# Decode attention on one core: a longer lag between scores and P·V, a plain load for q, and a loop on TensorE

## The chip, the cores and the metric

The kernel runs on one core of one Trainium2 chip. The metric is the device time of one execution in microseconds (us). Before the change the kernel took 352.61 us, the median of 4 runs (350.58 to 353.67 us). A profile is one further execution, recorded by the hardware; its span is 1.8 to 1.9 us shorter than the measured time of the same execution.

Engines are named as the profile names them: PE is TensorE (PEld its weight loads), DVE is VectorE, ACT is ScalarE, POOL is GpSimd, SP is SyncE. A trailing q (SPq, ACTq) means that engine's sequencer.

## The reference

```python
B, Hq, Hkv, Sq, Sk, D = 8, 32, 4, 4, 8192, 128        # bf16 inputs
k = jnp.repeat(k, Hq // Hkv, axis=1)
v = jnp.repeat(v, Hq // Hkv, axis=1)
scores = jnp.einsum("bhqd,bhkd->bhqk", q, k) * D ** -0.5
p = softmax(scores, axis=-1)
return jnp.einsum("bhqk,bhkd->bhqd", p, v)
```

Each batch has 128 query rows (32 heads x 4) in four groups of 32 that share a K/V head. K and V together are 134.22 MB and are read once; everything else is small.

## The kernel before

K and V come in 64 loads of 2,097,152 bytes ("units"), 32 each, all issued from SP. A unit holds 4 "chunks" of 512 positions for all four K/V heads; a batch has 16 chunks. There are four K buffers and four V buffers. For each chunk, PE transposes K (`ktp`), DVE and ACT each copy half of it out of PSUM (`kte`), PE computes scores (`qk`), and DVE scales them into SBUF and keeps a running minimum of the negated scores (`ev`). After 16 chunks of a batch its maximum is known (`negmax`), and the second half can begin: ACT computes the exponentials (`exp`), PE transposes them (`tp`), DVE copies (`ptc`), PE multiplies by V (`pv`).

The second half of a batch runs one batch, 16 chunks, behind its first half, so K is loaded 16 chunks ahead of V:

```python
for c in range(NCH):                      # NCH = 16
    steps.append((None, c))
for b in range(B):
    for c in range(NCH):
        n2 = b * NCH + c                                    # chunk of the second half
        n1 = (b + 1) * NCH + c if b + 1 < B else None       # chunk of the first half
        steps.append((n2, n1))
...
for (n2, n1) in steps:                    # order of the loads
    if n1 is not None and n1 % CPU == 0: dma_order.append(("k", n1 // CPU))
    if n2 is not None and n2 % CPU == 0: dma_order.append(("v", n2 // CPU))
...
# SP: a buffer is refilled when PE is done with what it held
if kind == "k":
    if m >= NK:  s.wait_ge(sem_pe_ktp, NPAIR * ((m - NK) * CPU + CPU))
    s.dma_start(Kn[ks][:, :, :], k[...]).then_inc(sem_k[ks], 16)
else:
    if m >= NVU: s.wait_ge(sem_pe_pv, (m - NVU) * CPU + CPU)
    s.dma_start(Vu[vs][:, :, :], v[...]).then_inc(sem_v[vs], 16)
...
# ACT, at the start: q is transposed by the DMA
for b in range(B):
    a.dma_start_transpose(QT[:, b, :], q[b].rearrange("h s d -> (h s) d")).then_inc(sem_q, 16)
...
# PE: the first score matmul waits for all of q (until 20.84 us in the profile); the K transposes behind it go on at 21.46 us
if first_qk[0]: t.wait_ge(sem_q, 16 * B)
...
# PE, after the last K: four chunks' transposes, then four chunks' P.V
for ui in range(0, len(tail_chunks), CPU):
    grp = tail_chunks[ui:ui + CPU]
    for n2 in grp:
        if n2 not in tp_done: emit_tp(n2)
    for n2 in grp: emit_pv(n2)
```

Of the kernel before, what the change touches and what calls it, by code (L numbers as in the profile page):

```python
# [5 lines left out]
dt = mybir.dt  # L6
# [5 lines left out]
def bass_standalone__gqa_softmax__sampling_kernel(  # L12
# [13 lines left out]
    P = 128  # L26
# [10 lines left out]

    NK = 4
# [4 lines left out]
    NPS = 16  # L43
    NTP = 2
    NPTS = 12
    GPB = 2
    NPAIR = G // GPB
    assert NPAIR == 2

# [3 lines left out]
    with ExitStack() as es:  # L53
# [5 lines left out]
        QT = sb("QT", [P, B, P], dt.bfloat16)  # L59
        Kn = [sb(f"Kn{i}", [P, G, JJ * D], dt.bfloat16) for i in range(NK)]  # L60
        Vu = [sb(f"Vu{i}", [P, G, JJ * D], dt.bfloat16) for i in range(NVU)]
        KT = [sb(f"KT{i}", [P, G, CH], dt.bfloat16) for i in range(NKT)]
        S_sb = sb("S", [P, Sk], dt.float32)
        Pb = [sb(f"P{i}", [P, CH], dt.bfloat16) for i in range(NPS)]
        PTs = [sb(f"PTs{i}", [P, CH], dt.bfloat16) for i in range(NPTS)]
# [10 lines left out]
        KT_ps = [ps_t(f"KTps{i}", [P, GPB, CH], dt.bfloat16) for i in range(NKTB)]  # L76

        sem_setup = sem("setup")
        sem_q = sem("qdma")
        sem_k = [sem(f"kdma{i}") for i in range(NK)]  # L80
# [16 lines left out]

        def kte_count(i):
            return i // NPAIR + 1

        steps = []
        for c in range(NCH):
            steps.append((None, c))
        for b in range(B):
            for c in range(NCH):
                n2 = b * NCH + c
                n1 = (b + 1) * NCH + c if b + 1 < B else None
                steps.append((n2, n1))
        NSTEPS = len(steps)
# [4 lines left out]
        def n1_of(t):  # L114
            return steps[t][1] if 0 <= t < NSTEPS else None

        TAIL_T = next((t for t, (n2, n1) in enumerate(steps) if n1 is None and n2 is not None), NSTEPS)

        def qk_deferred(n1):
            return (n1 % NCH) != NCH - 1  # L120

        def ktp_hoisted(t):
            if t <= 0 or t >= NSTEPS:
                return False
            n2, n1 = steps[t]
            return n1 is not None and n2 is not None and (n2 % NCH) == 0
# [30 lines left out]
        def _(s):  # L157
            for kind, m in dma_order:
# [19 lines left out]
        def _(t):  # L178
            t.wait_ge(sem_setup, 2)

            def emit_ktp(n1, pair):
# [3 lines left out]
                if cc == 0 and pair == 0:  # L185
                    t.wait_ge(sem_k[ks], 16 * (m // NK + 1))
                qi = n1 * NPAIR + pair
                qs = qi % NKTB
                if qi >= NKTB:
                    prev = qi - NKTB  # L190
                    if prev % NPAIR == 0:
                        t.wait_ge(sem_dve_kte, kte_count(prev))
                    else:
                        t.wait_ge(sem_act_kte, kte_count(prev))
# [11 lines left out]
            first_qk = [True]  # L206

            def emit_qk(n1):
                b, c = bc(n1)
                kt = n1 % NKT  # L210
                ss = n1 % NSP
                if first_qk[0]:
                    t.wait_ge(sem_q, 16 * B)
                    first_qk[0] = False
                t.wait_ge(sem_dve_kte, kte_count(n1 * NPAIR + 0))
                t.wait_ge(sem_act_kte, kte_count(n1 * NPAIR + 1))
                if n1 >= NSP:
                    t.wait_ge(sem_dve_p1, n1 - NSP + 1)
                for g in range(G):
                    ins = t.matmul(  # L220
                        S_ps[ss][32 * g:32 * (g + 1), :],
                        lhsT=QT[:, b, 32 * g:32 * (g + 1)],
# [6 lines left out]
            def emit_tp(n2):  # L229
                psl = n2 % NPS  # L230
                ts = n2 % NTP
                t.wait_ge(sem_act, n2 + 1)
                if n2 >= NTP:
                    t.wait_ge(sem_dve_pt, n2 - NTP + 1)
# [8 lines left out]
            def emit_pv(n2):  # L243
# [6 lines left out]
                t.wait_ge(sem_dve_pt, n2 + 1)  # L250
                if cc == 0:
                    t.wait_ge(sem_v[vs], 16 * (m // NVU + 1))
                if c == 0 and b >= 1:
                    t.wait_ge(sem_dve_fin, 3 * (b - 1) + 3)
# [14 lines left out]
            pending_qk = None  # L269
            tp_done = set()  # L270
            for ti in range(TAIL_T):
                n2, n1 = steps[ti]
                hoisted_here = ktp_hoisted(ti)
                if n1 is not None and not hoisted_here:
# [205 lines left out]
```

## Time and profile before

| | before |
|---|---|
| median time | 352.61 us |
| span of the profile | 351.2 us |
| K and V | 134.22 MB, 64 loads |
| GB/s in the middle (50 to 320 us) | 407 to 408 |
| busy share PE / DVE / ACT | 75% / 65% / 63% |

The first lines are from the page: the span; busy time by engine; what the DMA moved in 40 equal slices of the span (8.8 us each); then queues, with packets, MB, and the time their packets took as a share of 16 DMA engines' span. Queue q1 carries K and V, q10 the DMA transposes of q, and q8 instructions in packets of 16 KB.

```profile
span 351.2 us, 12106 instructions
...
PE 261.9 (75%) x5120; PEld 206.4 (59%) x5120; DVE 227.9 (65%) x544; ACT 222.3 (63%) x385; POOL 5.2 (1%) x14
...
GB/s 262 375 349 379 413 406 407 408 407 409 408 408 408 408 411 407 407 410 407 409 408 410 409 406 411 409 407 406 411 411 404 409 408 410 407 409 406 350 239 7
...
q1 hardware_dynamic: 33792, 134.22, 96.3%
q8 instruction: 41, 0.67, 0.8%
q10 hardware_dynamic: 1280, 0.26, 0.4%
```

No compute engine is above 75%, and the DMA moves a flat 408 GB/s from slice 6 to slice 37. The kernel is limited by its loads; the GB/s line falls off only at its two ends. The table of time windows looks closer there. Its columns are the window, its length, busy us (and instructions) of PE, PEld, DVE, ACT and POOL, the granted PE clock, the mean DMA share and GB/s.

```profile
4.00:8.78 4.78, 0.00 (x0) 0.00 (x0) 0.00 (x0) 0.00 (x0) 0.00 (x0) 1.00 1.06 338
...
22.00:26.30 4.30, 4.30 (x49) 3.33 (x47) 2.81 (x7) 1.88 (x2) 0.00 (x0) 1.00 0.81 323
26.30:30.70 4.40, 4.40 (x72) 3.30 (x69) 4.32 (x12) 3.24 (x4) 0.00 (x0) 1.00 0.94 344
...
200.00:300.00 100.00, 78.20 (x1528) 61.87 (x1525) 69.15 (x167) 66.79 (x118) 1.62 (x3) 0.91 1.03 408
...
325.00:330.00 5.00, 4.45 (x103) 3.29 (x101) 4.21 (x11) 3.78 (x5) 0.00 (x0) 0.96 0.87 348
330.00:335.00 5.00, 2.79 (x24) 1.54 (x28) 2.74 (x9) 3.56 (x11) 0.54 (x1) 0.72 0.98 376
335.00:338.00 3.00, 2.84 (x73) 2.38 (x73) 0.98 (x3) 3.00 (x10) 0.00 (x0) 0.50 0.76 309
338.00:340.00 2.00, 1.69 (x45) 1.26 (x46) 1.15 (x3) 2.00 (x7) 0.00 (x0) 0.74 0.55 215
```

Early, 338 GB/s at a DMA share above 1 (1.06) means that the DMA engines were busy. From 22 to 31 us the share falls to 0.81 and 0.94: the DMA had run short of issued loads, the fifth K load being issued only at 25.4 us. At the back the rate falls step by step.

The chain of work that ended last shows the end of the kernel (start in us, length in us, what):

```profile
331.44 7.79 ACT P L432 x21
...
339.32 2.83 ACT P L432 x8
...
346.50 1.10 PE acc L258 x64
...
347.68 0.36 DVE osb L368
...
348.32 0.54 POOL out_dram L149
```

After the last K, the 16 exponentials of the last batch run one after another on ACT; only then come the last transposes, P·V, normalization and store.

### The profile page before, as it was taken

What the parts mean: (1) busy time and instruction counts of PE and PEld (TensorE: products, weight loads), DVE (VectorE), ACT (ScalarE), POOL (GpSimd) and SP (SyncE); (2) the same over time, 40 slices, a digit from 0 to 9 for tenths busy, and PEclk for the clock granted to TensorE, in tenths of its full rate; (3) what the DMA queues carried; (4) which work ended last, traced back from release to release, by engine and by line L of the source; (5) the groups of instructions that cost most, each with busy time, mean ns of one, the idle gap of its engine ahead of it and who ended that gap; (6) DMA issues with size and microseconds to landing.
All of it is one profiled execution on the core that took longest, in us unless ns stands there. A gap on an engine that the chain in (4) does not pass through costs nothing.

```text
span 351.2 us, 12106 instructions
## 1 busy us (share of the span) xinstructions
PE 261.9 (75%) x5120; PEld 206.4 (59%) x5120; DVE 227.9 (65%) x544; ACT 222.3 (63%) x385; POOL 5.2 (1%) x14
## 2 busy tenths in 40 slices
PE   0469988886867979786698776978687879696774
PEld 0347666665645757564576655766565657475463
DVE  0139978876755778576758675777575686575743
ACT  0327697857756478485749575775575766665690
POOL 0000000000000000000000000000000000000000
PEclk9999999999988899899969998899899898988868
DMA  8999999999999999999999999999999999999950
GB/s 262 375 349 379 413 406 407 408 407 409 408 408 408 408 411 407 407 410 407 409 408 410 409 406 411 409 407 406 411 411 404 409 408 410 407 409 406 350 239 7
DMA packets 35380, 135.51 MB, mean 386 GB/s; under 512 B 2432, under 2 KB 2432, under 8 KB 35328
## 3 DMA queue, kind: packets, MB, share of 16 engines
q1 hardware_dynamic: 33792, 134.22, 96.3%
q8 instruction: 41, 0.67, 0.8%
q10 hardware_dynamic: 1280, 0.26, 0.4%
q0 software_dynamic: 256, 0.26, 0.2%
q14 instruction: 11, 0.09, 0.1%
HBM read 134.22 MB, written 0.26 MB: 383 GB/s over the span
## 4 chain that ended last, share of the span: by engine, by line
DMA 82%; PE 9%; ACT 3%; ACTq 3%; issue 1%; SPq 1%; DVE 1%; POOL 0%; DVEq 0%
DMA Vu<-in_v_dram 79%; PE KTps L199 5%; ACT P L432 3%; DMA QT<-in_q_dram 3%; ACTq L407 3%; PE Sps L220 2%; PE acc L258 1%; PE PTps L236 1%; SPq L164 1%; DVE PTs L351 0%; DVE KT L320 0%; POOL out_dram L149 0%; DVE osb L368 0%; DVE S L331 0%; DVE negmax L341 0%
## 5 line engine op out<-in xcount | busy, mean ns | idle before, releaser
L418 ACT ACTIVATE KT<-KTps 128x1024 bf16<-128x1024 bf16 x128 | 130.9, 1023 | 97.0 <-PE KTps L199 94.3
L199 PE MATMUL KTps<-ident,Kn 128*128 128x128 bf16 x2048 | 149.2, 231 | 14.4 <-DMA Kn<-in_k_dram 10.1
L199 PEld LDWEIGHTS KTps<-ident,Kn 128*128 128x128 bf16 x2048 | 131.9, 104 | 20.0 <-issue 20.0
L331 DVE TENSOR_SCALAR_CACHE_REDUCE S<-Sps 128x512 f32<-128x512 f32 x128 | 88.6, 692 | 31.8 <-PE Sps L220 22.4
L320 DVE COPY KT<-KTps 128x1024 bf16<-128x1024 bf16 x128 | 88.4, 691 | 23.4 <-PE KTps L199 22.6
L432 ACT ACTIVATE P<-S,negmax 128x512 bf16<-128x512 f32 x128 | 91.3, 713 | 11.9 <-DVE negmax L341 11.9
L351 DVE COPY PTs<-PTps 128x512 bf16<-128x512 bf16 x128 | 53.7, 422 | 62.8 <-PE PTps L236 62.0
L258 PE MATMUL acc<-Vu,PTs 128*32 128x128 bf16 x2048 | 54.4, 231 | 47.4 <-DMA Vu<-in_v_dram 34.0
L258 PEld LDWEIGHTS acc<-Vu,PTs 128*32 128x32 bf16 x2048 | 41.4, 101 | 66.2 <-issue 51.4
L220 PE MATMUL Sps<-KT,QT 128*32 128x512 bf16 x512 | 54.0, 409 | 12.9 <-DMA QT<-in_q_dram 7.2
L236 PE MATMUL PTps<-ident,P 128*128 128x128 bf16 x512 | 54.4, 235 | 10.9 <-ACT P L432 8.4
L236 PEld LDWEIGHTS PTps<-ident,P 128*128 128x128 bf16 x512 | 31.5, 103 | 26.6 <-ACT P L432 11.4
L220 PEld LDWEIGHTS Sps<-KT,QT 128*32 128x32 bf16 x512 | 13.5, 93 | 28.2 <-DMA QT<-in_q_dram 7.4
L432 ACT ACTIVATION_READ_ACCUMULATOR P<-S,negmax 128x1 f32 x128 | 24.4, 191 | 0.0
L331 DVE DVE_READ_ACCUMULATOR S<-Sps 128x1 f32 x128 | 10.7, 83 | 0.0
L149 POOL DMA_DIRECT2D out_dram<-osb x8 | 4.5, 558 | 342.9 <-DVE osb L368 342.9
L418 ACT ACT_TABLE_LOAD x1 | 1.3, 1283 | 11.6 <-issue 11.6
L368 DVE TENSOR_SCALAR osb<-acc,rrec 128x128 bf16<-128x128 f32 x8 | 2.8, 351 | 1.5 <-PE acc L258 1.3
L341 DVE TENSOR_REDUCE negmax<-rminp 128x1 f32<-128x16 f32 x8 | 1.4, 170 | 0.3
L363 DVE RECIPROCAL rrec<-rsum 128x1 f32<-128x1 f32 x8 | 1.3, 164 | 0.3
L359 DVE TENSOR_REDUCE rsum<-rsump 128x1 f32<-128x16 f32 x8 | 1.3, 161 | 0.0
L141 POOL TENSOR_SCALAR_AFFINE_SELECT ident<-ident 128x128 bf16<-128x128 bf16 x1 | 0.3, 284 | 0.2 <-POOL ident L139 0.2
(5 smaller groups left out, 0.6 us busy)
## 6 DMA issues: line engine op xcount, KB each, us to landing
Kn<-in_k_dram SPq DMA_DIRECT2D x32, 2048.0 KB, 24.2
Vu<-in_v_dram SPq DMA_DIRECT2D x32, 2048.0 KB, 24.3
out_dram<-osb POOLq DMA_DIRECT2D x8, 32.0 KB, 4.8
QT<-in_q_dram ACTq DMA_TRANSPOSE x8, 8.7
```

Source lines behind the costliest of these rows:

```text
L149: gp.dma_start(out[b].rearrange("h s d -> (h s) d"), out_sb[b % 2][:, :]).then_inc(sem_out[b % 2], 16)
L164: s.dma_start(Kn[ks][:, :, :], k[b, :, u * KUNIT:(u + 1) * KUNIT, :].rearrange("g (p jj) d -> p g (jj d)", jj=JJ),).then_inc(sem_k[ks], 16)
L199: ins = t.transpose(KT_ps[qs][:, gl, j * P:(j + 1) * P], Kn[ks][:, g, jj * D:(jj + 1) * D], ident[:, :],)
L220: ins = t.matmul(S_ps[ss][32 * g:32 * (g + 1), :], lhsT=QT[:, b, 32 * g:32 * (g + 1)], rhs=KT[kt][:, g, :], start=True, stop=True, tile_po ...
L236: ins = t.transpose(PT_ps[ts][:, j * P:(j + 1) * P], Pb[psl][:, j * P:(j + 1) * P], ident[:, :],)
L258: ins = t.matmul(acc[32 * g:32 * (g + 1), 0:D], lhsT=PTs[tsb][:, j * P + 32 * g:j * P + 32 * (g + 1)], rhs=Vu[vs][:, g, jj * D:(jj + 1) * ...
L320: vv.tensor_copy(KT[kt][:, 0:GPB, :], KT_ps[qs][:, :, :]).then_inc(sem_dve_kte, 1)
L331: vv.tensor_scalar(S_sb[:, c * CH:(c + 1) * CH], S_ps[ss][:, :], -scale, None, ALU.mult, ALU.min, accum_out=rowmin_parts[bp][:, c:c + 1],) ...
L351: vv.tensor_copy(PTs[tsb][:, :], PT_ps[ts][:, 0:CH]).then_inc(sem_dve_pt, 1)
L407: a.dma_start_transpose(QT[:, b, :], q[b].rearrange("h s d -> (h s) d")).then_inc(sem_q, 16)
L418: a.activation(KT[kt][:, GPB:2 * GPB, :], KT_ps[qs][:, :, :], ACT.Copy).then_inc(sem_act_kte, 1)
L432: a.activation(Pb[psl][:, :], S_sb[:, c * CH:(c + 1) * CH], ACT.Exp, bias=negmax[bp][:, :], scale=-1.0, accum_out=rowsum_parts[bp][:, c:c ...
```

## The change

The intent is to shorten both ends. The lag grows from 16 to 24 chunks, so that six V loads follow the last K and hide the last exponentials. Scores are kept in a ring of 24 chunks; P and P-transposed buffers shrink to 8 each to pay for it. q comes by one plain load in front of the K loads and is transposed on PE. PE's middle part becomes a hardware loop of 6 trips over 16 steps, with waits that count up by the trip number. The core of the diff:

```diff
+    L = NCH + NCH // 2
+    NSS = L
-    NPS = 16
+    NPS = 8
-    NPTS = 12
+    NPTS = 8
...
+        NSTEPS = NTOT + L
         steps = []
-        for c in range(NCH):
-            steps.append((None, c))
-        for b in range(B):
-            for c in range(NCH):
-                n2 = b * NCH + c
-                n1 = (b + 1) * NCH + c if b + 1 < B else None
-                steps.append((n2, n1))
+        for t in range(NSTEPS):
+            n1 = t if t < NTOT else None
+            n2 = t - L if t >= L else None
+            steps.append((n2, n1))
...
+            s.dma_start(Qn, q.rearrange("b h s d -> (h s) b d")).then_inc(sem_q, 16)
...
+            t.wait_ge(sem_q, 16)
+            for b in range(B):
+                ins = t.transpose(QT_ps[:, b * P:(b + 1) * P], Qn[:, b, :], ident[:, :])
+            ins.then_inc(sem_qt, 1)
...
+            for ti in range(L):
+                step(ti)
+            with t.Fori(0, TRIPS) as trip:
+                loop[0] = trip
+                off[0] = trip * NCH
+                for ti in range(L, L + NCH):
+                    step(ti)
...
-            for b in range(B):
-                a.dma_start_transpose(
-                    QT[:, b, :], q[b].rearrange("h s d -> (h s) d")
-                ).then_inc(sem_q, 16)
```

Cut: a two-slot copy of the current batch's q (so that the loop body names fixed addresses), changed slot tables for K-transposed buffers, and the removal of special orders at batch ends.

More of the change, by code (lines that the diff above doesn't have):

```diff
@@ L48, in bass_standalone__gqa_softmax__sampling_kernel @@
     assert NPAIR == 2
+    assert B * D <= NPTS * CH
+    assert B * P <= 2 * CH
     NTOT = B * NCH
@@ L59, in bass_standalone__gqa_softmax__sampling_kernel @@
         QT = sb("QT", [P, B, P], dt.bfloat16)
+        QTc = sb("QTc", [P, 2, P], dt.bfloat16)
         Kn = [sb(f"Kn{i}", [P, G, JJ * D], dt.bfloat16) for i in range(NK)]
@@ L62, in bass_standalone__gqa_softmax__sampling_kernel @@
         KT = [sb(f"KT{i}", [P, G, CH], dt.bfloat16) for i in range(NKT)]
-        S_sb = sb("S", [P, Sk], dt.float32)
+        S_sb = sb("S", [P, NSS, CH], dt.float32)
         Pb = [sb(f"P{i}", [P, CH], dt.bfloat16) for i in range(NPS)]
-        PTs = [sb(f"PTs{i}", [P, CH], dt.bfloat16) for i in range(NPTS)]
+        PTs_all = sb("PTs", [P, NPTS, CH], dt.bfloat16)
+        PTs = [PTs_all[:, i, :] for i in range(NPTS)]
+        nq_slots = -(-(B * D) // CH)
+        Qn = PTs_all[:, 0:nq_slots, :].rearrange("p a c -> p (a c)")[:, 0:B * D].rearrange(
+            "p (b d) -> p b d", b=B
+        )
         rowmin_parts = [sb(f"rminp{i}", [P, NCH], dt.float32) for i in range(2)]
@@ L76, in bass_standalone__gqa_softmax__sampling_kernel @@
         KT_ps = [ps_t(f"KTps{i}", [P, GPB, CH], dt.bfloat16) for i in range(NKTB)]
+        QT_ps = S_ps[0][:, :].bitcast(dt.bfloat16)
         sem_setup = sem("setup")
         sem_q = sem("qdma")
+        sem_qt = sem("qt")
         sem_k = [sem(f"kdma{i}") for i in range(NK)]
@@ L96, in bc, with ktslot, ktprev, kslot @@
             return n // NCH, n % NCH
+        KSLOT = [i % NKTB for i in range(NPAIR * NCH - 2)] + [0, 1]
+        KTSLOT = [c % NKT for c in range(NCH - 1)] + [1]
+        def ktslot(n1):
+            return KTSLOT[n1 % NCH]
+        def ktprev(n1):
+            p = n1 - 1
+            while p >= 0 and ktslot(p) != ktslot(n1):
+                p -= 1
+            return p
+        def kslot(qi):
+            return KSLOT[qi % (NPAIR * NCH)]
+        def kprev(qi):
+            p = qi - 1
+            while p >= 0 and kslot(p) != kslot(qi):
+                p -= 1
+            return p
         def kte_count(i):
             return i // NPAIR + 1
+        NSTEPS = NTOT + L
         steps = []
-        for c in range(NCH):
-            steps.append((None, c))
-        for b in range(B):
-            for c in range(NCH):
-                n2 = b * NCH + c
-                n1 = (b + 1) * NCH + c if b + 1 < B else None
-                steps.append((n2, n1))
-        NSTEPS = len(steps)
+        for t in range(NSTEPS):
+            n1 = t if t < NTOT else None
+            n2 = t - L if t >= L else None
+            steps.append((n2, n1))
         def n2_of(t):
             return steps[t][0] if 0 <= t < NSTEPS else None
-        def n1_of(t):
-            return steps[t][1] if 0 <= t < NSTEPS else None
-        TAIL_T = next((t for t, (n2, n1) in enumerate(steps) if n1 is None and n2 is not None), NSTEPS)
-        def qk_deferred(n1):
-            return (n1 % NCH) != NCH - 1
-        def ktp_hoisted(t):
-            if t <= 0 or t >= NSTEPS:
-                return False
-            n2, n1 = steps[t]
-            return n1 is not None and n2 is not None and (n2 % NCH) == 0
+        TAIL_T = NTOT
+        tail_chunks = [steps[ti][0] for ti in range(TAIL_T, NSTEPS)]
+        tail_units = []
+        for n2 in tail_chunks:
+            if n2 // CPU not in tail_units:
+                tail_units.append(n2 // CPU)
         dma_order = []
@@ L179, in _ @@
             t.wait_ge(sem_setup, 2)
+            t.wait_ge(sem_q, 16)
+            for b in range(B):
+                ins = t.transpose(QT_ps[:, b * P:(b + 1) * P], Qn[:, b, :], ident[:, :])
+            ins.then_inc(sem_qt, 1)
+            loop = [None]
+            off = [0]
             def emit_ktp(n1, pair):
@@ L185, in emit_ktp @@
                 if cc == 0 and pair == 0:
-                    t.wait_ge(sem_k[ks], 16 * (m // NK + 1))
+                    t.wait_ge(sem_k[ks], 16 * (m // NK + 1) + off[0])
                 qi = n1 * NPAIR + pair
-                qs = qi % NKTB
-                if qi >= NKTB:
-                    prev = qi - NKTB
+                qs = kslot(qi)
+                prev = kprev(qi)
+                if prev // NPAIR >= n1 - 1 and prev >= 0:
                     if prev % NPAIR == 0:
-                        t.wait_ge(sem_dve_kte, kte_count(prev))
+                        t.wait_ge(sem_dve_kte, kte_count(prev) + off[0])
                     else:
-                        t.wait_ge(sem_act_kte, kte_count(prev))
+                        t.wait_ge(sem_act_kte, kte_count(prev) + off[0])
                 for gl in range(GPB):
@@ L204, in emit_ktp @@
                 ins.then_inc(sem_pe_ktp, 1)
-            first_qk = [True]
             def emit_qk(n1):
                 b, c = bc(n1)
-                kt = n1 % NKT
+                kt = ktslot(n1)
                 ss = n1 % NSP
-                if first_qk[0]:
-                    t.wait_ge(sem_q, 16 * B)
-                    first_qk[0] = False
-                t.wait_ge(sem_dve_kte, kte_count(n1 * NPAIR + 0))
-                t.wait_ge(sem_act_kte, kte_count(n1 * NPAIR + 1))
+                if n1 == 0:
+                    t.wait_ge(sem_qt, 2)
+                t.wait_ge(sem_dve_kte, kte_count(n1 * NPAIR + 0) + off[0])
+                t.wait_ge(sem_act_kte, kte_count(n1 * NPAIR + 1) + off[0])
                 if n1 >= NSP:
-                    t.wait_ge(sem_dve_p1, n1 - NSP + 1)
+                    t.wait_ge(sem_dve_p1, n1 - NSP + 1 + off[0])
                 for g in range(G):
@@ L221, in emit_qk @@
                         S_ps[ss][32 * g:32 * (g + 1), :],
-                        lhsT=QT[:, b, 32 * g:32 * (g + 1)],
+                        lhsT=QTc[:, c // (NCH // 2), 32 * g:32 * (g + 1)],
                         rhs=KT[kt][:, g, :],
@@ L231, in emit_tp @@
                 ts = n2 % NTP
-                t.wait_ge(sem_act, n2 + 1)
-                if n2 >= NTP:
+                t.wait_ge(sem_act, n2 + 1 + off[0])
+                if loop[0] is None and n2 >= NTP:
                     t.wait_ge(sem_dve_pt, n2 - NTP + 1)
@@ L249, in emit_pv @@
                 bp = b % 2
-                t.wait_ge(sem_dve_pt, n2 + 1)
+                t.wait_ge(sem_dve_pt, n2 + 1 + off[0])
                 if cc == 0:
-                    t.wait_ge(sem_v[vs], 16 * (m // NVU + 1))
-                if c == 0 and b >= 1:
-                    t.wait_ge(sem_dve_fin, 3 * (b - 1) + 3)
+                    t.wait_ge(sem_v[vs], 16 * (m // NVU + 1) + off[0])
+                if c == 0 and (b >= 1 or loop[0] is not None):
+                    t.wait_ge(sem_dve_fin, 3 * b + (0 if loop[0] is None else loop[0] * 3))
                 for j in range(JB):
@@ L267, in emit_pv, with step @@
                 ins.then_inc(sem_pe_pv, 1)
-            pending_qk = None
             tp_done = set()
-            for ti in range(TAIL_T):
+            state = {"pending": None}
+            def step(ti):
+                pending_qk = state["pending"]
                 n2, n1 = steps[ti]
-                hoisted_here = ktp_hoisted(ti)
-                if n1 is not None and not hoisted_here:
-                    emit_ktp(n1, 0)
-                if ti == 0 and n2_of(0) is not None:
-                    emit_tp(n2_of(0))
-                    tp_done.add(n2_of(0))
-                if n1 is not None and not hoisted_here:
-                    emit_ktp(n1, 1)
+                emit_ktp(n1, 0)
+                emit_ktp(n1, 1)
                 if pending_qk is not None:
                     emit_qk(pending_qk)
-                    pending_qk = None
+                state["pending"] = n1
                 if n2 is not None:
                     emit_pv(n2)
-                if n1 is not None:
-                    if qk_deferred(n1):
-                        pending_qk = n1
-                    else:
-                        emit_qk(n1)
-                if ktp_hoisted(ti + 1):
-                    emit_ktp(n1_of(ti + 1), 0)
-                    emit_ktp(n1_of(ti + 1), 1)
                 nx2 = n2_of(ti + 1)
@@ L297, in _ @@
                     tp_done.add(nx2)
+            TRIPS = (TAIL_T - L) // NCH
+            for ti in range(L):
[5 more added lines that the diff above has]
+                    step(ti)
+            loop[0] = None
+            off[0] = 0
+            state["pending"] = L + NCH * TRIPS - 1
+            for n2 in range(NCH * TRIPS + 1):
+                tp_done.add(n2)
+            for ti in range(L + NCH * TRIPS, TAIL_T):
+                step(ti)
+            pending_qk = state["pending"]
             if pending_qk is not None:
@@ L300, in _ @@
                 pending_qk = None
-            tail_chunks = [steps[ti][0] for ti in range(TAIL_T, NSTEPS)]
-            for ui in range(0, len(tail_chunks), CPU):
-                grp = tail_chunks[ui:ui + CPU]
+            for u in tail_units:
+                grp = [n2 for n2 in tail_chunks if n2 // CPU == u]
                 for n2 in grp:
@@ L312, in _ @@
         def _(vv):
+            vv.wait_ge(sem_qt, 1)
+            for h in range(2):
+                vv.tensor_copy(QTc[:, h, :], QT_ps[:, 0:P])
+            vv.tensor_copy(QT[:, :, :], QT_ps[:, 0:B * P]).then_inc(sem_qt, 1)
+            vv.wait_ge(sem_qt, 2)
             def emit_kte(n1):
-                kt = n1 % NKT
+                kt = ktslot(n1)
                 qi = n1 * NPAIR + 0
-                qs = qi % NKTB
+                qs = kslot(qi)
                 vv.wait_ge(sem_pe_ktp, qi + 1)
-                if n1 >= NKT:
-                    vv.wait_ge(sem_pe_qk, n1 - NKT + 1)
+                if ktprev(n1) >= 0:
+                    vv.wait_ge(sem_pe_qk, ktprev(n1) + 1)
                 vv.tensor_copy(KT[kt][:, 0:GPB, :], KT_ps[qs][:, :, :]).then_inc(sem_dve_kte, 1)
@@ L325, in emit_ev @@
                 ss = n1 % NSP
+                sslot = n1 % NSS
+                if c == NCH // 2 + 1 and b + 1 < B:
+                    vv.tensor_copy(QTc[:, 0, :], QT[:, b + 1, :])
+                if c == 1 and b >= 1:
+                    vv.tensor_copy(QTc[:, 1, :], QT[:, b, :])
                 vv.wait_ge(sem_pe_qk, n1 + 1)
-                if b >= 1:
-                    vv.wait_ge(sem_act, (b - 1) * NCH + c + 1)
+                if n1 >= NSS:
+                    vv.wait_ge(sem_act, n1 - NSS + 1)
                 if c == 0 and b >= 2:
@@ L331, in emit_ev @@
                 vv.tensor_scalar(
-                    S_sb[:, c * CH:(c + 1) * CH],
+                    S_sb[:, sslot, :],
                     S_ps[ss][:, :],
@@ L350, in emit_ptc @@
                     vv.wait_ge(sem_pe_pv, n2 - NPTS + 1)
-                vv.tensor_copy(PTs[tsb][:, :], PT_ps[ts][:, 0:CH]).then_inc(sem_dve_pt, 1)
+                vv.tensor_copy(PTs[tsb], PT_ps[ts][:, 0:CH]).then_inc(sem_dve_pt, 1)
             def emit_fin(b):
@@ L374, in _ @@
                 n2, n1 = steps[ti]
-                hoisted_here = ktp_hoisted(ti)
-                if hoisted_here:
-                    emit_kte(n1)
                 if n2 is not None:
                     emit_ptc(n2)
-                if n1 is not None and not hoisted_here:
-                    emit_kte(n1)
+                emit_kte(n1)
                 if pending_ev is not None:
                     emit_ev(pending_ev)
-                    pending_ev = None
-                if n1 is not None:
-                    if qk_deferred(n1):
-                        pending_ev = n1
-                    else:
-                        emit_ev(n1)
+                pending_ev = n1
                 if n2 is not None:
@@ L396, in _ @@
                 pending_ev = None
-            for ti in range(TAIL_T, NSTEPS):
-                n2 = steps[ti][0]
-                emit_ptc(n2)
-                b, c = bc(n2)
-                if c == NCH - 1:
-                    emit_fin(b)
+            fin_pending = []
+            for u in tail_units:
+                grp = [n2 for n2 in tail_chunks if n2 // CPU == u]
+                for n2 in grp:
+                    emit_ptc(n2)
+                for fb in fin_pending:
+                    emit_fin(fb)
+                fin_pending = []
+                for n2 in grp:
+                    b, c = bc(n2)
+                    if c == NCH - 1:
+                        fin_pending.append(b)
+            for fb in fin_pending:
+                emit_fin(fb)
         @block.scalar
         def _(a):
-            for b in range(B):
-                a.dma_start_transpose(
-                    QT[:, b, :], q[b].rearrange("h s d -> (h s) d")
-                ).then_inc(sem_q, 16)
             def emit_kte(n1):
-                kt = n1 % NKT
+                kt = ktslot(n1)
                 qi = n1 * NPAIR + 1
-                qs = qi % NKTB
+                qs = kslot(qi)
                 a.wait_ge(sem_pe_ktp, qi + 1)
-                if n1 >= NKT:
-                    a.wait_ge(sem_pe_qk, n1 - NKT + 1)
+                if ktprev(n1) >= 0:
+                    a.wait_ge(sem_pe_qk, ktprev(n1) + 1)
                 a.activation(
@@ L425, in emit_exp @@
                 psl = n2 % NPS
+                sslot = n2 % NSS
                 if c == 0:
@@ L433, in emit_exp @@
                     Pb[psl][:, :],
-                    S_sb[:, c * CH:(c + 1) * CH],
+                    S_sb[:, sslot, :],
                     ACT.Exp,
@@ L439, in emit_exp @@
                 ).then_inc(sem_act, 1)
-            if n2_of(0) is not None:
-                emit_exp(n2_of(0))
-            for ti, (n2, n1) in enumerate(steps):
+            for ti in range(NSTEPS):
+                n2, n1 = steps[ti]
                 nxt = n2_of(ti + 1)
-                exp_first = nxt is not None and (nxt % NCH) != 0
-                if exp_first:
+                if nxt is not None:
                     emit_exp(nxt)
@@ L449, in _ @@
                     emit_kte(n1)
-                if nxt is not None and not exp_first:
-                    emit_exp(nxt)
 _INS = ['q', 'k', 'v']
```

## The prediction

> **What bounds the kernel now.** The DMA. The page's queue table shows 134.22 MB of K and V on one hardware queue, 96.3% of 16 engines' span. By windows, 50 to 320 us runs at 407 to 408 GB/s with DMA share 1.02 to 1.03, while PE is busy about 78% of that stretch, DVE 70%, ACT 68%. The chain of waits is 79% V loads. [...]this trace's 408 decides, and I take 408 as the ceiling. So only the ends can give time.
>
> - Front (windows): 4 to 22 us moves 338 to 381 GB/s, while eight DMA transposes of q run until 20.8 us (chain). Against 408 about 0.76 MB is missing, 1.9 us. From 22 to 30.7 us only 323 and 344 GB/s: the fifth K load was issued only at 25 us (timeline), because PE stood behind the score matmul that waited for QT. About 0.65 MB, 1.6 us.
> - Back (windows): from 325 to 342 us the rate falls 348, 376, 309, 215, 84: about 1.8 MB, 4.4 us missing. The last batch's exponentials start only after the last K (331.44 us), run 10.7 us on ACT, and release V buffers late. Data ends at about 342, the span at 351.2.
>
> **What the change does.** It lags P·V by 24 chunks instead of 16, so the last six V loads (6 x 2.1 MB / 408 = 31 us) follow the last K. The 24 exponentials left (0.90 us each, 21.6 us) hide under them. The tail shrinks to: last V lands, 64 P·V matmuls (1.1 us), normalization, store, end: 4.7 us, as from 346.50 us to the end now. It replaces the DMA transposes by one plain load of 256-byte rows plus eight PE transposes and three DVE copies (about 1 us, under the first K load). [...]estimating 1 us of DMA, 0.9 of the 1.9 us comes back. PE's middle becomes a loop of 6 trips. [...]PE has about 22% of 41 us = 9 us spare per trip[...]. If the body stays resident, the instruction queue (41 packets, 0.8% of the span) shrinks: I count 0.8 us.
>
> **Sum.** Last data: 342 - 1.6 - 4.4 - 0.9 - 0.8 = 334.3 us. Add 1 to 1.5 us for completion and engine skew, 4.7 us of tail: span 340.3. Measured times exceed spans by 1.3 to 1.8 us. Predicted 341.5 us (-3.2%), range 337 to 346. Faster by over 2%: 0.84; within 2%: 0.14; slower: 0.02.
>
> **What would show it.** Right: 408 GB/s from about 10 us to the last slice; the chain ends with V load, P·V, osb, out; ACT idle at the end; no wait of exp for negmax; fewer instruction-queue packets. First K lands near 9 to 10 us.
>
> **What would make it wrong.** The steady rate moves (loop refetch, or fewer instruction bytes than counted). The early 338 to 381 GB/s is not the transposes but a slow start of its own. The small-row q load costs several us in front of K0. A PE stall at each branch exceeds the slack and empties the DMA queue. The 16 engines end unevenly.

That a stall at the branch, if there was one, would stay hidden in PE's 9 us of slack per trip was the expectation. 342 - 1.6 - 4.4 - 0.9 - 0.8 = 334.3 us, with 1.3 us (of the "1 to 1.5") and 4.7 us added 340.3 us. The 0.9 us rests on the estimate of 1 us for the q load alone; for comparison, the 1,280 packets of q's transposes (q10) took 24.5 us in the profile of before, 1.5 us for each of 16 engines.

## The result, and the profile after

The changed kernel is correct. Its median is 345.92 us (10 runs, 344.41 to 348.0); the kernel before, in the same rounds, 352.23 us (15 runs). The ratio is 0.9816, with a 95% interval from 0.9789 to 0.9844. Ratios here are the mean time of one kernel's fast runs over that of the other's of the same rounds, so not quite the ratio of the medians. The time lies inside the predicted range, just below its upper end of 346: 6.3 us were gained where 11 were forecast. Four of the ten runs lie above 346 us. The gain is clear of noise, but "faster by over 2%", to which the prediction gave 0.84, is not shown: the interval of the ratio reaches to both sides of 0.98.

The same views of the changed kernel. The page:

```profile
span 345.3 us, 12239 instructions
...
GB/s 280 414 409 409 407 409 408 408 409 407 408 409 410 409 409 410 409 410 410 410 410 410 410 409 407 409 409 409 409 412 409 409 409 410 409 407 376 378 283 9
...
q1 hardware_dynamic: 34832, 134.48, 97.9%
q8 instruction: 15, 0.25, 0.3%
```

The windows:

```profile
4.00:8.78 4.78, 0.73 (x7) 0.46 (x5) 0.95 (x3) 0.00 (x0) 0.00 (x0) 1.00 1.02 409
...
22.00:26.30 4.30, 4.30 (x69) 3.29 (x66) 4.25 (x13) 3.27 (x4) 0.00 (x0) 1.00 1.03 411
...
315.00:320.00 5.00, 3.69 (x112) 2.49 (x109) 3.55 (x10) 4.95 (x14) 0.00 (x0) 1.00 0.90 352
320.00:325.00 5.00, 2.01 (x55) 1.42 (x59) 1.59 (x4) 5.00 (x15) 0.00 (x0) 0.85 0.95 354
325.00:330.00 5.00, 3.55 (x73) 2.80 (x72) 2.29 (x7) 4.73 (x14) 0.41 (x1) 0.50 1.02 387
330.00:335.00 5.00, 4.30 (x104) 3.40 (x98) 1.70 (x4) 2.71 (x7) 0.13 (x1) 0.50 0.85 334
335.00:338.00 3.00, 2.77 (x64) 2.09 (x60) 1.25 (x3) 0.33 (x2) 0.00 (x0) 0.65 0.09 38
```

And the end of the chain:

```profile
322.28 2.59 issue
...
329.44 1.90 PE acc L289 x49
...
334.20 1.82 PE acc L289 x33
...
340.65 1.04 PE acc L289 x64
341.77 0.36 DVE osb L416
342.13 0.28 issue
342.41 0.54 POOL out_dram L174
```

The front is repaired: 409 GB/s from 4 us on. The instruction queue fell from 41 packets to 15. The back is not what was forecast: the rate still falls from 315 us on, and the chain runs through PE, which stood still for 2.59 us, ran at half clock (0.50) for ten, and began the last P·V at 340.65 us. How much of this delay is the pause and how much the clock is not separated.

To see the back properly, a mean over 16 DMA engines is not enough. Each load's semaphore counts to 16 in the kernel, and the trace has 16 landing records for each load, 9.4 us from the first to the last for load 60 of the kernel before. I call what leaves one record a ring and take it that there is one for each of the 16 DMA engines of the page; the records name neither, so that the last ring is the same one from load to load is my reading too. PE waits for the full count: in e9 the last P·V began 0.14 us after the last record. The landing records give, in us from the start of the span (the zero of all views here), the first and the last ring of the last five loads:

```
load            60             61             62             63             64     span ends
before   312.9 / 322.3  318.0 / 327.4  323.1 / 332.4  328.2 / 337.6  336.5 / 342.5     351.2
changed  310.7 / 317.6  315.8 / 322.7  322.7 / 327.8  328.5 / 333.1  333.9 / 338.2     345.3
```

The expectations quoted below were written with landing times 0.2 to 0.3 us later than these, and so with tails that much shorter (338.5 and 6.8 us for the changed kernel, where the trace has 338.2 and 7.1). Differences between runs are hardly touched.

In the kernel before, the fastest ring is 9.4 us ahead of the slowest, and it is the fastest that is held up at the end (328.2 to 336.5 us). The slowest ring lands a load every 5.0 to 5.2 us right to the end, as fast as ever. So the falling rate in the windows was fast rings waiting, while the slowest, which decides when data is complete, was never short of work. The lag builds up over the run: 1.2 us at the first K, 3.1 us at the 9th load, 9.4 us from the 57th to the 63rd. In the changed kernel it is 1.9 us at the 9th load and 6.9 us near the end. There it grows in steps. Three of them, of 0.7 to 1.0 us each (loads 33, 41 and 49), fall in the stretches in which an output store landed (at 175.5, 214.6 and 257.6 us), with no packet of PE's instructions (q8) between 87.1 and 301.5 us. So PE's packets are not the only small traffic that comes with a step. Packets of the page's other instruction queue, q14, fall in the same stretches (at 172.4, 212.5 and 258.7 us), and no run removed them or the stores.

### The profile page after: what moved, and what is told of

Its sections match the earlier page's. It is cut to its first block, busy times and chain, and to the rows that moved or that the text cites. A ratio compares the mean times of both kernels' runs of the same rounds, so it can differ in the third digit from the quotient of the medians.

```text
span 345.3 us, 12239 instructions
## 1 busy us (share of the span) xinstructions
PE 268.6 (78%) x5128; PEld 212.7 (62%) x5128; DVE 228.0 (66%) x561; ACT 222.0 (64%) x385; POOL 5.1 (1%) x14
## 4 chain that ended last, share of the span: by engine, by line
DMA 82%; PE 14%; issue 2%; DVE 1%; SPq 0%; POOL 0%; DVEq 0%
DMA Vu<-in_v_dram 79%; PE KTps L233 6%; PE acc L289 3%; PE PTps L267 3%; DMA Kn<-in_k_dram 2%; PE Sps L251 2%; DVE PTs L399 1%; SPq L190 0%; DVE osb L416 0%; POOL out_dram L174 0%; SPq L183 0%; DVE rrec L411 0%; DVE rsum L407 0%; DVE S L379 0%; DVE negmax L389 0%
## 5 line engine op out<-in xcount | busy, mean ns | idle before, releaser
L233 PE MATMUL KTps<-ident,Kn 128*128 128x128 bf16 x2048 | 152.3, 234 | 5.6 <-DMA Kn<-in_k_dram 5.4
L233 PEld LDWEIGHTS KTps<-ident,Kn 128*128 128x128 bf16 x2048 | 134.9, 106 | 11.5 <-DMA Kn<-in_k_dram 6.1
L289 PE MATMUL acc<-Vu,PTs 128*32 128x128 bf16 x2048 | 55.2, 240 | 60.3 <-DMA Vu<-in_v_dram 55.1
L289 PEld LDWEIGHTS acc<-Vu,PTs 128*32 128x32 bf16 x2048 | 42.3, 106 | 79.4 <-issue 68.5
L267 PE MATMUL PTps<-ident,P 128*128 128x128 bf16 x512 | 55.5, 240 | 3.1 <-DVE PTs L399 2.1
L251 PE MATMUL Sps<-KT,QTc 128*32 128x512 bf16 x512 | 54.2, 410 | 0.4 <-issue 0.3
L267 PEld LDWEIGHTS PTps<-ident,P 128*128 128x128 bf16 x512 | 32.6, 105 | 19.0 <-issue 6.5
L251 PEld LDWEIGHTS Sps<-KT,QTc 128*32 128x32 bf16 x512 | 13.3, 93 | 15.1 <-DVE KT L361 3.1
L208 PE MATMUL Sps<-ident,PTs 128*128 128x128 bf16 x8 | 1.0, 305 | 3.7 <-DMA PTs<-in_q_dram 3.7
L208 PEld LDWEIGHTS Sps<-ident,PTs 128*128 128x128 bf16 x8 | 0.8, 137 | 3.7 <-issue 3.7
```

Source lines behind the costliest of these rows:

```text
L208: ins = t.transpose(QT_ps[:, b * P:(b + 1) * P], Qn[:, b, :], ident[:, :])
L233: ins = t.transpose(KT_ps[qs][:, gl, j * P:(j + 1) * P], Kn[ks][:, g, jj * D:(jj + 1) * D], ident[:, :],)
L251: ins = t.matmul(S_ps[ss][32 * g:32 * (g + 1), :], lhsT=QTc[:, c // (NCH // 2), 32 * g:32 * (g + 1)], rhs=KT[kt][:, g, :], start=True, sto ...
L267: ins = t.transpose(PT_ps[ts][:, j * P:(j + 1) * P], Pb[psl][:, j * P:(j + 1) * P], ident[:, :],)
L289: ins = t.matmul(acc[32 * g:32 * (g + 1), 0:D], lhsT=PTs[tsb][:, j * P + 32 * g:j * P + 32 * (g + 1)], rhs=Vu[vs][:, g, jj * D:(jj + 1) * ...
```

## The experiments

Each experiment ran on the chip beside the kernel before. For e1 to e12 the mean takes in the profiled execution, which the ratio leaves out. The last two columns come from the run's one profile: the last V's landing on the first and on the last ring, and the time from the latter to the end of the span (the "tail").

| run | mean us | ratio to before (95%) | last landing, first / last ring | tail us |
|---|---|---|---|---|
| before | 352.37 | | 336.5 / 342.5 | 8.7 |
| changed | 345.89 | 0.9816 (0.9789 to 0.9844) | 333.9 / 338.2 | 7.1 |
| e1 front only | 349.59 | 0.9933 (0.9891 to 0.9976) | 332.1 / 339.3 | 6.9 |
| e2 old q | 348.55 | 0.9894 (0.9858 to 0.9929) | 337.2 / 342.1 | 4.9 |
| e3 unrolled | 346.47 | 0.9840 (0.9807 to 0.9873) | 332.5 / 339.0 | 5.0 |
| e4 tail order | 344.94 | 0.9795 (0.9762 to 0.9827) | 334.6 / 337.9 | 4.9 |
| e5 V in K buffers | 345.81 | 0.9829 (0.9794 to 0.9863) | 330.9 / 337.8 | 4.9 |
| e6 lag 20 | 345.32 | 0.9806 (0.9772 to 0.9840) | 331.1 / 337.9 | 5.7 |
| e7 one load in two parts | 357.88 | 1.0166 (1.0128 to 1.0204) | | |
| e8 = e4 + e5 | 345.42 | 0.9804 (0.9771 to 0.9837) | 331.0 / 337.8 | 6.8 |
| e9 changed, again | 345.13 | 0.9802 (0.9767 to 0.9836) | 332.9 / 337.9 | 4.9 |
| e10 = e4, unrolled | 346.58 | 0.9836 (0.9807 to 0.9865) | 336.6 / 340.3 | 5.1 |
| e11 = e4, last store from SP | 343.35 | 0.9748 (0.9719 to 0.9778) | 335.3 / 337.9 | 3.6 |
| e12 = e11, last V in halves | 344.82 | 0.9783 (0.9752 to 0.9814) | 336.5 / 338.9 | 5.1 |

### e1: only the front of the change

```diff
 # the kernel before, with
+            s.dma_start(Qn[:, :, :], q.rearrange("b h s d -> (h s) b d")).then_inc(sem_q, 16)
+            for b in range(B):
+                ins = t.transpose(QT_ps[:, b * P:(b + 1) * P], Qn[:, b, :], ident[:, :])
+            vv.tensor_copy(QT[:, :, :], QT_ps[:, 0:B * P]).then_inc(sem_qt, 1)
-                a.dma_start_transpose(...)
```

> The kernel before with only the q load changed (one plain load, eight PE transposes, one copy). My theory now: the change's gain in DMA time is all at the front. In the landing records of before the 9th of the 64 K/V loads has landed on all rings at 55.9 us, in the changed kernel at 51.7 us, and both then need 286.8 us for the other 55. So this run should land its 9th load near 52 us, its last near 338.5 us, and be about 4 us (1.2%) faster than before, ratio 0.986 to 0.991, with the tail after the last landing as before, 8 to 9 us. Rival (the prediction's own sizes): the front is worth 2.5 us, ratio 0.993, and the rest comes from the deeper lag.

The 9th load landed at 52.3 us as I expected, but the last only at 339.3 us, and the mean time fell by 2.7 us (352.25 in the same rounds to 349.59). My theory that the front is nearly all of it missed; the rival, the prediction's own 2.5 us for the front, hit.

### e2: the change without its front

```diff
 # the changed kernel, with
-            s.dma_start(Qn, ...)            # and the eight PE transposes
+            for b in range(B): a.dma_start_transpose(QT[:, b, :], ...)
+                if ti == 1:                 # DVE, before the first scores
+                    vv.wait_ge(sem_q, 16 * B); vv.tensor_copy(QTc[:, 0, :], QT[:, 0, :]); ...
```

> The changed kernel with the eight DMA transposes of q put back; lag 24, rings, PE loop stay. My theory: only the shorter tail is left, about 1.5 to 2 us (ratio 0.994 to 0.998), the last landing at 341 to 343 us. Rival (the prediction): the lag and the loop are worth 8.5 us of the 11 by themselves, ratio near 0.976; scaled to the measured total, at least 4 us, ratio 0.988.

The last landing, 342.1 us, is as I expected, only 0.4 us before that of the kernel before. The time is not: 3.7 us are gained, close to the rival's 4 us. What I had wrong was the tail: it is 4.9 us here, and I had taken the 7.1 us of the changed kernel's one profile for typical (see e9).

### e3: the loop written out

```diff
-            with t.Fori(0, TRIPS) as trip:
-                ...
+            for ti in range(TAIL_T):
+                step(ti)
```

> The changed kernel with PE's loop written out. The instruction queue should go back from 15 to about 41 packets. If fewer instruction packets matter for the slowest of the 16 rings, its lag behind the fastest at the end grows from 6.9 us to about 9 us, and the run is 1 to 2.5 us slower than the changed kernel (ratio to before 0.985 to 0.989). Rival: the two kernels need the same 286.8 us for the last 55 loads whatever the packets, so the loop is worth nothing: ratio within 0.3% of 0.982. If the stall of 2.6 us in PE's tail (322.3 us) comes from leaving the loop, it is gone here; if it is ordinary instruction fetch it stays somewhere in the tail.

The page's line of the instruction queue:

```profile
q8 instruction: 41, 0.67, 0.8%
```

With 41 packets the last V landed at 339.0 us, 0.8 us after that of the changed kernel, and the slowest ring was 8.7 us behind near the end, in place of 6.9. The mean time rose by 0.6 us against the changed kernel, by 1.3 us against its repetition e9. That alone is near the noise: the ratio, 0.984, is short of the 0.985 to 0.989 of my theory and lies within the rival's 0.3% of 0.982. e10 repeats it. The landing records also speak for the rival: the 0.8 us was there at the 9th load already (52.2 us against 51.5), when both kernels had fetched the same four packets, and from there to the last load both took 286.8 us. So the lag grew as expected, but that it cost this time is not shown. The stall in PE's tail did not go: waits of 1.9 us for "issue" remain in the tail here, so leaving the loop was not its cause.

Waits of PE from 50 to 310 us show whether the loop's branch costs anything. This line (who waited for whom; us in total, times, the longest) is from the changed kernel:

```profile
PE acc L289 <- issue: 1.4, 2, 0.8
```

and this one from e3, unrolled:

```profile
PE acc L289 <- issue: 7.5, 4, 2.8
```

The loop has fewer stalls than the straight code. All nine packets that the changed kernel fetched before the loop's end came before 88 us; the next came at 301.5 us. So the six trips of a body of 1,280 matmul and weight-load instructions ran without one packet of this queue in more than 210 us.

### e4: another order in the tail

```diff
-                for n2 in grp:
-                    if n2 not in tp_done: emit_tp(n2)
-                for n2 in grp: emit_pv(n2)
+            tps(grps[0])
+            for i, grp in enumerate(grps):
+                if i + 1 < len(grps): tps(grps[i + 1])
+                for n2 in grp: emit_pv(n2)
```

> The changed kernel, but in the tail PE transposes the P of the next unit before the P.V of this one, so that only 64 P.V matmuls wait for the last V. My theory: PE is behind the V loads in the tail (last V landed at 338.5 us, its P.V began at 340.65 us) because each unit's transposes, copies and P.V run in series after the V wait of the unit before; this order gives 1.5 to 2 us: the last P.V starts within 0.3 us of the last landing, ratio to before about 0.976 to 0.978. Rival: the backlog comes from the 2.6 us stall and the half clock, which the order does not touch: gain under 0.7 us.

In this profile the last P·V begins 0.14 us after the last landing, and the mean is 0.95 us under the changed kernel's. But e9 shows the unchanged order doing the same, with a mean of 345.13 us, 0.2 us from e4. So a gain from the order is not shown, and my expectation of 1.5 to 2 us missed.

### e5: the last V loads into K buffers

```diff
+                    late = m >= NUNITS - NK                  # the last four V units
+                    if late: s.wait_ge(sem_pe_ktp, NPAIR * (m * CPU + CPU))
-                    if m >= NVU:
+                    elif m >= NVU:
                         s.wait_ge(sem_pe_pv, (m - NVU) * CPU + CPU)
-                    s.dma_start(Vu[vs][:, :, :], ...)
+                    s.dma_start((Kn[m % NK] if late else Vu[vs])[:, :, :], ...)
```

> The changed kernel, but the last four V loads go into K buffers, which are free by then, so they are issued without waiting for P.V. In the changed kernel the windows from 315 to 335 us show 352, 354, 387, 334 GB/s. Rival theory (the prediction's reading of such a dip): the DMA starves for V buffers, so this gives 1.5 to 2.5 us and the last V lands at 336 to 337 us. My theory: the dip is only the 15 faster rings waiting; the slowest ring was never short of work (its landings stay 5.1 to 5.3 us apart), so the first ring ends about 3 us earlier but the last landing stays at 338.5 us within 0.5 us, and the time within 0.2% of the changed kernel.

This experiment decides how the falling rate is to be read. Its windows:

```profile
315.00:320.00 5.00, 3.30 (x93) 2.40 (x92) 3.29 (x11) 5.00 (x15) 0.00 (x0) 1.00 1.03 411
320.00:325.00 5.00, 2.39 (x80) 1.66 (x77) 1.27 (x5) 5.00 (x17) 0.00 (x0) 1.00 1.02 406
325.00:330.00 5.00, 3.59 (x80) 3.18 (x80) 1.87 (x7) 3.72 (x12) 0.54 (x1) 0.50 1.02 406
330.00:335.00 5.00, 4.43 (x139) 3.33 (x141) 3.10 (x8) 2.83 (x8) 0.00 (x0) 0.82 0.51 202
```

The dip is gone: 411, 406, 406 GB/s where the changed kernel had 352, 354, 387. The fastest ring ends at 330.9 us, 3.0 us earlier. The slowest ends at 337.8 us, within 0.4 us of the changed kernel and 0.1 us of e9, and the time is the same. A dip was removed in full, and nothing was gained.

### e6: a lag of 20 chunks

```diff
-    L = NCH + NCH // 2
+    L = NCH + NCH // 4
```

> The changed kernel with a lag of 20 chunks in place of 24. My theory: the lag is not worth DMA time, and its tail gain is mostly there as soon as some V loads follow the last K: last landing within 0.5 us of 338.5 us, time within 0.3% of the changed kernel. Rival (lag is the main lever, V loads behind the last K hide the exponentials): 5 V loads (25.7 us) still cover 20 exponentials (18 us), but the time lies between the lags of 16 and 24, about 1 to 2 us slower.

As my theory had it: last landing 337.9 us, mean 345.32 us, not distinguishable from the lag of 24. The score ring could be four chunks smaller at no cost.

### e7: one load in two parts, to take one ring out of it

```diff
-                    s.dma_start(Vu[vs][:, :, :], src).then_inc(sem_v[vs], 16)
+                    for p0, p1 in ([(0, 120), (120, 128)] if m == 27 else [(0, 128)]):
+                        s.dma_start(Vu[vs][p0:p1, :, :], src[p0:p1, :, :]).then_inc(sem_v[vs], 16)
```

> The changed kernel with one V load (unit 27) split by partitions: [...]. If one ring is the slow one and it is ring 15, the lag of the slowest ring in the landings after that load falls from about 6.9 us to the second slowest's 3.5 us, and the last V lands 2 to 3 us earlier. If the slow ring is another, it gets the same or up to 0.7 us more and the time is unchanged or up to 0.5 us longer. If instead the aggregate bandwidth sets the end, no change.

This failed as a test. Which rings the parts of 120 and 8 partitions would use was assumed. The landing records show only that the two parts left 15 + 8 records and one more each, where two whole loads leave 32; whether ring 15 was left out they do not say. And the stream ran at about half speed from 305 to 325 us (178 to 244 GB/s). Windows before and during it:

```profile
295.00:300.00 5.00, 3.75 (x96) 3.14 (x96) 3.84 (x9) 3.33 (x7) 0.34 (x1) 1.00 1.02 408
...
310.00:315.00 5.00, 5.00 (x63) 4.23 (x65) 2.85 (x6) 1.72 (x3) 0.00 (x0) 0.53 1.02 201
```

The DMA share stays at 1.02 while the rate halves: single packets of 4096 bytes took 320 ns at the median (305 to 320 us), against 159 to 164 ns elsewhere. The run was 5.8 us slower than the kernel before. Which ring is the slowest, and why the stream slowed down with these two parts, stay open.

### e8: e4 and e5 together

Its edit is the two diffs above in one kernel.

> Both the tail order of e4 and the K buffers for the last V loads of e5. If my theory holds, it is as e4 alone, 1.5 to 2 us faster than the changed kernel (ratio to before about 0.976 to 0.978). If the V buffers starve the DMA, the two gains add to 3 to 4 us (0.972).

Two gains that add would have shown 0.972; measured were 0.9804 and a last landing of 337.8 us. That agrees with e5, and again nothing is gained by the tail order: in this profile PE stalled twice in the tail, for 2.0 and 2.8 us, and the tail was 6.8 us long.

### e9: the changed kernel once more

No edit.

> The changed kernel once more, unaltered, on the same chip as the next three. Its runs so far lie between 344.4 and 348.0 us, and its profiled run (345.3 us span, clock 0.889) had 6.8 us from the last landing to the end, where e4 and e5 had 4.7 us. If the tail's backlog is a matter of the granted clock and of instruction fetch in PE's tail, this kernel scatters by more than 2 us again, and a profile with a higher clock there has a tail under 6 us. If the backlog is there in every run, the tail is near 6.8 us again.

Five of its six runs lie between 344.45 and 345.09 us, one at 347.05. The end of this profile's chain:

```profile
324.58 13.32 DMA Vu<-in_v_dram
337.90 0.14 issue
338.04 1.10 PE acc L289 x64
339.14 0.03 DVEq L415
339.17 0.05 issue
339.22 0.36 DVE osb L416
```

Here PE waits for the DMA, as the prediction wanted, and the tail is 4.9 us. In the first profile PE was late; its granted clock was 0.50 from 325 to 335 us, where e9 has 0.50 and then 0.90 (330 to 335 us). So the 7.1 us tail of the first profile was one of several outcomes. In both profiles PE also stood still once for 2.6 to 2.7 us in the tail (the "issue" pieces at 322.28 and 321.10 us). An instruction packet began at 322.6 us in the first and at 321.3 us in the second, inside the stall. In e3 (packet 329.3 us, stall from 329.9 us), e4 (328.6, from 327.9) and e8 (323.8 and 330.1, from 324.3 and 329.8) a packet, about 1 us long, overlaps the stall too. That these stalls are waits for instructions is read from this coincidence; no run removed them alone. Single waits of PE for "issue" in the tail, 1.9 to 3.1 us long, stand in eight of the nine profiles with the loop (all but e6, 1.1 us; e7 left out), and of 1.9 and 2.5 us in e3 and e10, without it.

### e10: the loop written out, with e4's tail

The edits are those of e3 and e4.

> e4 (tail order changed) with PE's loop written out: the loop's worth with the tail's scatter taken out of it. The unrolled run e3 landed its last V at 339.2 us against 338.1 to 338.5 us in the runs with the loop. If the extra instruction packets cost the slowest ring that, this run is 0.7 to 1.2 us slower than e4, 345.7 to 346.2 us. If the loop is worth nothing, it is within 0.3 us of e4.

The mean is 1.6 us above e4's (on another chip; the kernel before had 352.2 us on both), and the slowest ring was 10.1 us behind the fastest near the end. The loss is a little more than expected. The profiled run was the slowest of the six and its first K landed late (10.95 us against 9.05 us in e4), so its last landing, 340.3 us, overstates it. Over all profiles with q loaded plainly, the last V landed at 337.8 to 338.2 us in the seven with the loop and unsplit loads, and at 339.0, 339.3 and 340.3 us in the three without the loop. But most of that difference is old: the 9th load landed at 51.3 to 51.6 us in the seven and at 52.2, 52.3 and 53.4 us in the three. From the 9th load to the last, the seven took 286.2 to 286.8 us, the three 286.8 to 287.1 us, so some 0.4 us can be the packets of the unrolled code. Why its first loads land late stays open.

### e11 and e12: a faster version

e11 is e4 with the last of the eight stores issued from SP:

```diff
-            for b in range(B):          # GpSimd
+            for b in range(B - 1):
...
+            s.wait_ge(sem_dve_fin, 3 * B)                 # SP, after its last load
+            s.dma_start(out[B - 1]..., out_sb[(B - 1) % 2][:, :]).then_inc(sem_last, 16)
+            s.wait_ge(sem_last, 16)
```

> e4 with the last output stored from SyncE's queue in place of GpSimd's. In e4 the profile has 0.28 us of issue, 0.54 us of GpSimd and then 2.4 us until the end of the span after the last normalization. [...]0.3 to 1 us faster than e4. If the end of the span is not set by the store's landing, no change.

The mean fell by 1.6 us against e4, to 343.35 us, more than expected. The page's lines of DMA issues (last column: the median us from issue to landing) seem to show why:

```profile
out_dram<-osb POOLq DMA_DIRECT2D x7, 32.0 KB, 5.1
out_dram<-osb SPq DMA_DIRECT2D x1, 32.0 KB, 1.5
```

But the 5.1 us is the median of stores among the K and V loads. The last store, behind all loads, took only 1.7 us in e4 as well. In both profiles the last normalization began at 339.2 us. From there the records of the last store and of the engine that issues it give, in us:

```
                store issued   landed   the engine's closing DRAIN   span ends
e4, from POOL         339.87   341.59             341.82 to 342.54      342.76
e11, from SP          339.61   341.08             341.26 to 341.26      341.47
```

So of the 1.3 us between these spans, 0.26 us is an earlier issue, 0.25 us a quicker landing, and 0.78 us lies after the landing: POOL closes with an instruction named DRAIN that took 0.72 us at the very end in e4 (0.71 us in the profiles of before and changed); in e11 POOL ran it at 333.3 us, beside other work. This kernel beats both: 0.9748 of the kernel before.

e12 also cuts the last V load in two, with two semaphores:

```diff
+                        for h in range(2):
+                            s.dma_start(Vu[vs][:, :, h * hw:(h + 1) * hw],
+                                        src[:, :, h * hw:(h + 1) * hw]).then_inc(sem_vl[h], 16)
```

> e11 with the last V load cut into two halves along the sequence, each with its own semaphore, so that only two of the four last P.V chunks (0.55 us of 1.1 us) wait for the last landing. Expected 0.3 to 0.6 us faster than e11, unless the 2 KB rows of the halves make that load slower than 5.1 us, in which case no gain or a loss.

It lost 1.5 us against e11. The halves landed at 335.8 and 338.9 us, so the second was 1.0 us later than the whole load in e11 (337.9 us), and PE stalled in the tail for 4.5 us in all, the last time from 337.3 to 339.3 us, past the last landing. The loss that the expectation allowed for came true; whether the rows of 2 KB had a part in it, beside the stalls, is not shown.

## Why the prediction was right or wrong

The time was inside the range and the direction right, but the gain was 6.3 us and not 11. That the time fell inside the range, by 0.08 us, is owed to the range's width: the largest term of the sum, the back, did not come. Chained means sort it into parts: front 2.7 us (before to e1), lag 3.1 us (e1 to e3), loop 0.9 us (e3 to the 16 runs of the changed kernel, mean 345.6 us). Their sum is 6.7 us. e3 differs from e1 in all that goes with the lag, rings of buffers and order included; the loop's part alone is near the noise and rests on e10 as well. A lag of 16 in the new kernel was not run, so what the lag alone is worth is not shown; a lag of 20 did as well as 24 (e6).

- **Front, 1.6 + 0.9 = 2.5 us forecast.** Right. e1 measured 2.7 us (its ratio's interval allows 0.8 to 3.8), and putting the transposes back in e2 cost 2.9 us. The plain q load's 1,024 packets took 18.2 us in all, 1.1 us for each of 16 rings, against the estimate of 1 us. The slow rate from 4 to 22 us was the transposes: it is 409 GB/s without them and 362 and 340 GB/s again in e2's slices 3 and 4. First K: 9.7 us, forecast 9 to 10.
- **Loop, 0.8 us forecast.** Right in size: 0.9 us (e3), 1.6 us (e10 against e4). How it comes about is not shown. There are fewer instruction packets (one took 1.1 us at the median) and a smaller lag (6.9 to 7.2 us near the end in the profiles with 15 packets, 8.7 to 10.2 us in those with 41), but from the 9th load on that is some 0.4 us of the last landing; the rest stands in the first loads (e10). A stall at the branch was not seen: PE's "issue" waits for P·V from 50 to 310 us came to 1.4 us, against 7.5 us unrolled (e3).
- **Back, "4.4 us missing" from the falling rate of 325 to 342 us.** This is the step that failed. It treated the mean rate of 16 rings as if all were short of work. The slowest ring was not, so nothing was there to gain. e1 and e3 differ in the lag, and their last landings by only 0.3 us (339.3 and 339.0). e5 removed such a dip and moved the last landing by at most 0.4 us, within what the unaltered kernel shows (338.2 and 337.9).
- **"Add 1 to 1.5 us for completion and engine skew."** Too small. The skew was 6.9 us at load 60 and 4.3 us at the last, and it was there to be read in the trace of before, as 9.4 us. The prediction's own list of what would make it wrong ends with "The 16 engines end unevenly"; it was not looked up.
- **Tail, 4.7 us after the last V.** Right, as a floor: 4.7 us from the start of the last P·V, 4.9 us from the landing, in e2, e4, e5 and e9, against 8.7 us before and 6.9 us in e1. In the first profile of the changed kernel PE was late and it was 7.1 us. The exponentials did hide, and no wait for negmax is left.
- **"408 GB/s to the last slice."** Wrong: the last full slices show 376, 378, 283. As e5 shows, that costs nothing.

So most of the lag's 3.1 us lies after the last landing (a tail of 5.0 us in e3, 6.9 in e1, 8.7 before), and only some 0.3 us before it. One profile of each is behind this: those of e1 and e3 differ by 2.2 us, and e1's was its fastest execution, so the remaining 0.9 us is not located.

## What to carry to other kernels

When one stream of loads bounds a kernel, look at when each load's last part lands and how far apart the loads' completions are; a falling mean rate near the end may only be the faster rings waiting or having finished, as here, where e5 removed the dip (352 to 411 GB/s) and moved the last landing by at most 0.4 us. Reordering work behind the last load paid here through the tail after the last landing (8.7 us before, 4.9 us in e9), so size it by that tail and not by missing bytes. Look at the ends too: here a loop on PE, with 15 instruction packets in place of 41, was worth 0.9 to 1.6 us, and issuing the last store from another engine 1.6 us, about half of what the longer lag brought.
